# Moving the wo projection into the next unit's step, and cutting the last w2 rows into pieces of 5, 3 and 1

## Chip, cores, metric

One core of one Trainium2 chip. The metric is device time in microseconds (us) of one execution. The kernel before takes 137.39 us, the median of four runs between 137.38 and 137.50. The profile's span is 135.6 us; the rest lies outside it.

## The reference, cut to what matters

```python
xn = layernorm(x)                                   # x: 2 x 576
return x + attention(xn, k_cache, v_cache, wq, wo) + mlp(xn, w1, b1, w2, b2)

# attention: 32 query heads, 16 KV heads of 128, the last 2048 keys of the cache
# mlp: (relu(xn @ w1 + b1) ** 2) @ w2 + b2, hidden size 4608
```

Everything is bf16. One token for each of two sequences meets 53.6 MB of weights and cache: 16.8 MB each for K and V, 4.7 MB for wq and for wo, 5.3 MB for w1 and for w2.

## The kernel before

The work on the cache is cut into eight units (four KV heads of one sequence each). A unit is a step: 64 transposes of K on TensorE, copies of the transposed K out of PSUM, 64 score matmuls, a softmax over VectorE, GpSimd and ScalarE. PV of an earlier unit is mixed in. After two units (a head group) the wo projection follows: a select of eight matmuls and a sum of sixteen.

```python
    def wo_proj(tq):
        ...                                   # rr = oG * rmask; 8 select matmuls; ws = copy
        wo_sb = wo_tiles.pop(tq)
        for r in range(WR):                   # 8 rows, two matmuls each
            out_acc(ws[:, r, :], lambda a, z: wo_sb[:, r, a:z])

    def mlp_o(s, r0, r1, last=False):         # one w2 piece: two matmuls a row
        w2_sb = w2_tiles.pop((s, r0))
        for r in range(r0, r1):
            o = (r - r0) * D
            out_acc(mlp["h"][:, s * FR + r, :], lambda a, z: w2_sb[:, o + a:o + z], stop=...)

    W2P = [(0, 0, 9), (0, 9, 18), (1, 0, 9), (1, 9, 15), (1, 15, 18)]
    ...
    for u in range(2, NU + 2):
        if u < NU:
            step(u)
        else:
            for g in range(NG): pv(u - 2, g)
        ...
        if u - 2 >= 1 and (u - 2) % B == B - 1:
            wo_proj((u - 2) // B)
        ...                                   # load_v(u), wo, load_k(u + 2); w2 pieces at the last unit
    for i, w in enumerate(W2P):
        mlp_o(*w, last=(i == len(W2P) - 1))
    # cast of the PSUM sum to bf16, two stores
```

All loads but those of x, b1 and b2, which are small, go through one queue of the sync engine, in program order. K, V and w2 share a pool of six buffers, so a load waits for the last reader of the buffer that it takes (in the profiled run of the kernel before, the issues of K and V waited 17.0 us for transposes and 7.9 us for PV).

## Time and profile before

| | before |
|---|---|
| time, median of 4 | 137.39 us |
| span of the profiled run | 135.6 us |
| bytes by the load queue, rate from slice 2 to 37 | 53.61 MB, about 420 GB/s |
| last byte landed / final cast starts | 132.26 / 132.87 us |
| spread of the 16 completions of the last piece | 3.36 us |

The top of the page of the kernel before: busy time, share of the span and number of instructions of each engine, and the granted TensorE clock in tenths, in 40 slices of 3.4 us.

```profile
span 135.6 us, 4461 instructions
PE 102.5 (76%) x2054; PEld 91.9 (68%) x2054; DVE 53.9 (40%) x124; ACT 43.0 (32%) x47; POOL 10.0 (7%) x31
...
PEclk9999985569855685556985698698559959955599
```

No compute engine is full. A 76% busy TensorE with a mean granted clock of 0.76, which is half clock for about 48% of the span, is near enough to its limit to be watched. The DMA row, which the prediction shows, is full. The completion times in this text are the trace's semaphore updates. A load has 16 of them here, as many as the core has DMA engines. I read each as that of one engine; the records carry no engine number. A load counts as landed with the last: the last piece's 16 run from 128.90 to 132.26 us, and the first matmul on it begins at 132.30.

### The profile page before, as it was taken

The numbers are of one execution on the slowest core, as the hardware profiler recorded it, in microseconds if no ns is written. First come the engines' busy times: TensorE is split into PE (matmuls) and PEld (weight loads), VectorE is DVE, ScalarE is ACT, GpSimd is POOL, SyncE is SP. The second block draws the span as 40 slices with busy tenths as digits, with TensorE's granted clock in tenths as the row PEclk, the third lists the DMA queues.
The fourth block names the chain that finished last, engine by engine and source line by source line (L and its number), as shares of the span: only waits on it lengthen the run. The fifth ranks groups of instructions, "written<-read, shape, count | busy, mean of one in ns | idle before, by whom it ended". The sixth has DMA issues, their size and how long they took to land.

```text
span 135.6 us, 4461 instructions
## 1 busy us (share of the span) xinstructions
PE 102.5 (76%) x2054; PEld 91.9 (68%) x2054; DVE 53.9 (40%) x124; ACT 43.0 (32%) x47; POOL 10.0 (7%) x31
## 2 busy tenths in 40 slices
PE   1049947599968999879943993999399599768961
PEld 0039947589968999839933993688399479664530
DVE  7502421574352325422653446355634645660001
ACT  6705550165012521004701550272155127110000
POOL 6400000110110001100011001101100110110000
PEclk9999985569855685556985698698559959955599
DMA  5999999999999999999999999999999999999940
GB/s 112 418 419 418 428 442 402 420 429 440 430 393 430 438 411 409 444 425 396 440 440 406 445 420 425 404 443 423 425 430 413 430 415 426 422 410 417 393 166 1
DMA packets 5278, 53.90 MB, mean 397 GB/s; under 512 B 630, under 2 KB 652, under 8 KB 1164
## 3 DMA queue, kind: packets, MB, share of 16 engines
q1 hardware_dynamic: 5188, 53.61, 94.7%
q8 instruction: 16, 0.26, 0.8%
q0 software_dynamic: 64, 0.01, 0.0%
q14 instruction: 2, 0.02, 0.0%
q10 hardware_dynamic: 8, 0.00, 0.0%
HBM read 53.62 MB, written 0.00 MB: 395 GB/s over the span
## 4 chain that ended last, share of the span: by engine, by line
DMA 55%; PE 35%; DVE 3%; issue 2%; POOL 1%; ACT 1%; SPq 1%; POOLq 0%; ACTq 0%
DMA k<-in_A_k_cache_dram 41%; PE kT_ps L237 18%; DMA w<-in_B_w_dram 10%; PE hT_ps L323 5%; DMA b_sb<-in_B_b_dram 4%; PE sc_ps L252 4%; PE out_ps L213 4%; PE oT_ps L289 3%; PE qT_ps L225 1%; ACT kT L240 1%; POOL b_sb L146 1%; DVE l L271 1%; DVE sub L266 1%; SPq L94 0%; DVE fin_sb L414 0%
## 5 line engine op out<-in xcount | busy, mean ns | idle before, releaser
L237 PE MATMUL kT_ps<-ident,k 128*128 128x128 bf16 x512 | 47.3, 260 | 9.9 <-DMA k<-in_A_k_cache_dram 9.9
L237 PEld LDWEIGHTS <-k 128*128 128x128 bf16 x512 | 39.6, 119 | 11.8 <-DMA k<-in_A_k_cache_dram 10.7
L240 ACT COPY kT<-kT_ps 128x1024 bf16<-128x1024 bf16 x32 | 32.3, 1012 | 40.1 <-PE kT_ps L237 40.0
L242 DVE COPY kT<-kT_ps 128x1024 bf16<-128x1024 bf16 x32 | 22.0, 690 | 33.4 <-PE kT_ps L237 33.4
L252 PE MATMUL sc_ps<-qT_all,kT 128*128 128x8 bf16 x512 | 21.6, 168 | 1.6 <-ACT kT L240 0.8
L252 PEld LDWEIGHTS <-kT 128*128 128x128 bf16 x512 | 19.1, 100 | 2.6 <-ACT kT L240 1.2
L289 PE MATMUL oT_ps<-pT,v 128*128 128x8 bf16 x512 | 15.5, 167 | 1.9 <-issue 1.4
L269 ACT ACTIVATE pT<-sub 128x512 bf16<-128x512 f32 x8 | 5.0, 630 | 35.1 <-DVE sub L266 35.1
L289 PEld LDWEIGHTS <-v 128*128 128x128 bf16 x512 | 14.4, 99 | 2.1 <-issue 1.6
L271 DVE TENSOR_REDUCE l<-pT 128x8 f32<-128x512 bf16 x8 | 8.5, 1066 | 4.2 <-ACT pT L269 4.2
L213 PE MATMUL out_ps<-wo,ws 128*2 128x288 bf16 x64 | 8.3, 438 | 2.4 <-DVE ws L309 2.4
L323 PE MATMUL hT_ps<-xnT,w 128*128 128x2 bf16 x144 | 9.8, 201 | 0.0
L323 PEld LDWEIGHTS <-w 128*128 128x128 bf16 x144 | 9.4, 165 | 0.0
L258 DVE TENSOR_REDUCE m<-sc_ps 128x8 f32<-128x512 f32 x8 | 5.5, 692 | 9.7 <-PE sc_ps L252 9.7
L262 POOL PARTITION_ALL_REDUCE gmax<-m x8 | 2.9, 364 | 84.8 <-DVE m L260 84.8
L213 PE MATMUL out_ps<-w,hT_sb 128*2 128x288 bf16 x72 | 6.9, 353 | 1.3 <-DMA w<-in_B_w_dram 1.3
L213 PEld LDWEIGHTS <-ws 128*2 128x2 bf16 x64 | 3.5, 115 | 5.4 <-DVE ws L309 2.8
L213 PEld LDWEIGHTS <-hT_sb 128*2 128x2 bf16 x72 | 3.8, 103 | 4.3 <-issue 1.9
L266 DVE TENSOR_TENSOR sub<-sc_ps,gm 128x512 f32<-128x512 f32 x8 | 5.5, 692 | 0.3
L225 PE MATMUL qT_ps<-xnT,wq 128*128 128x2 bf16 x128 | 4.0, 165 | 2.2 <-DMA wq<-in_A_wq_dram 1.9
L225 PEld LDWEIGHTS <-wq 128*128 128x128 bf16 x128 | 3.9, 103 | 2.2 <-DMA wq<-in_A_wq_dram 2.0
L273 POOL PARTITION_ALL_REDUCE lsum<-l x8 | 3.2, 398 | 24.5 <-DVE l L271 24.5
(58 smaller groups left out, 35.1 us busy)
## 6 DMA issues: line engine op xcount, KB each, us to landing
v<-in_A_v_cache_dram SPq DMA_DIRECT2D x8, 2048.0 KB, 28.4
k<-in_A_k_cache_dram SPq DMA_DIRECT2D x7, 2048.0 KB, 29.4
w<-in_B_w_dram SPq DMA_DIRECT2D x4, 1152.0 KB, 17.7
wo<-in_A_wo_dram SPq DMA_DIRECT2D x4, 1152.0 KB, 27.4
wq<-in_A_wq_dram SPq DMA_DIRECT2D x4, 1024.0 KB, 6.9
w<-in_B_w_dram SPq DMA_DIRECT2D x3, 1296.0 KB, 22.7
k<-in_A_k_cache_dram SPq DMA_DIRECT2D x2, 1024.0 KB, 9.1
w<-in_B_w_dram SPq DMA_DIRECT2D x1, 864.0 KB, 15.7
```

What stands on the lines that cost most here:

```text
L213: nc.tensor.matmul(out_ps[32 * i:32 * i + B, :], lhsT=lhsT, rhs=rhs_of(i * OH, (i + 1) * OH), start=start, stop=stop, skip_group_check=True)
L225: nc.tensor.matmul(qT_ps[:, h, :], lhsT=lhsT, rhs=xnT[:, xc, :], start=(c == 0 and h == 0), stop=(c == KC - 1), skip_group_check=True)
L237: nc.tensor.transpose(out=kT_ps[:, i * P:(i + 1) * P], in_=k_sb[:, j * Dh:(j + 1) * Dh], identity=ident[:])
L240: nc.scalar.copy(out=kT[:], in_=kT_ps[:])
L242: nc.vector.tensor_copy(out=kT[:], in_=kT_ps[:])
L252: nc.tensor.matmul(sc_ps[:, g * JG + i, :], lhsT=kT[:, i * P:(i + 1) * P], rhs=qT_all[:, b, tq * NC:(tq + 1) * NC], start=True, stop=True)
L258: nc.vector.tensor_reduce(out=m1[:], in_=sc_ps[:].rearrange("p j c -> p c j"), axis=AX.X, op=ALU.max)
L266: nc.vector.tensor_tensor(out=sub[:], in0=sc_ps[:], in1=gm2[:].unsqueeze(1).to_broadcast([P, NJ, NC]), op=ALU.subtract)
L269: nc.scalar.activation(out=pT[:], in_=sub[:], func=ACT.Exp, scale=scale)
L271: nc.vector.tensor_reduce(out=l1[:], in_=pT[:].rearrange("p j c -> p c j"), axis=AX.X, op=ALU.add)
L289: nc.tensor.matmul(oT_ps[:], lhsT=v_sb[:, j * Dh:(j + 1) * Dh], rhs=pT_tiles[u][:, j, :], start=(j == 0), stop=(j == NJ - 1))
L323: nc.tensor.matmul(hT_ps[:, s * FR + r, :], lhsT=lhsT, rhs=xnT[:, xc, :], start=(c == 0 and s == 0 and r == 0), stop=(c == KC - 1), skip_g ...
```

## The change

Its intent is to take work off the end: the wo projection of a finished head group moves into a later step, the PV of the last units moves ahead of it, and the last loads become smaller, so that little is left to compute after the last byte. The core of the diff, with cuts marked:

```diff
-    W2P = [(0, 0, 9), (0, 9, 18), (1, 0, 9), (1, 9, 15), (1, 15, 18)]
+    W2P = [(0, 0, 9), (0, 9, 18), (1, 0, 9), (1, 9, 14), (1, 14, 17), (1, 17, 18)]
...
-    def wo_proj(tq):
+    def wo_sel(tq):            # the select; wo_acc(tq) has the 16 matmuls of the sum
...
-    def step(u, extra=()):
+    def step(u, hooks):
...
+            for f in hooks.get(g, ()):
+                f()
...
+    for u in range(2, NU):
+        hooks = {}
+        if u >= 4 and u % B == 0:
+            hooks = {3: [lambda t=u // B - 2: wo_sel(t)], 6: [lambda t=u // B - 2: wo_acc(t)]}
+        step(u, hooks)
...
+    for w in W2P:
+        issue_w2(*w)
+    for g in range(NG):
+        pv(NU - 2, g)
+    wo_sel(NQ - 2)
+    wo_acc(NQ - 2)
+    for g in range(NG):
+        pv(NU - 1, g)
+    mlp_o(*W2P[0])
+    wo_sel(NQ - 1)
+    mlp_o(*W2P[1])
+    wo_acc(NQ - 1)
+    for i in range(2, len(W2P)):
+        mlp_o(*W2P[i], last=(i == len(W2P) - 1))
```

Beside this the loads of b1 and b2 and the matmuls of x and b2 are written later, and a PSUM tile is cleared.

More of the change, by code (lines that the diff above doesn't have):

```diff
@@ L61 @@
     FR = L1 // P
-    NFC = S * FR
+    CH = [(s * L1 + r, FR, P) for s in range(S) for r in range(FR)]
+    NFC = len(CH)
     OH = D // 2
@@ L110, in issue_w1, with w_operands @@
         issue_w(w1_tiles, B_w1, c, "w1", F, L1)
-    def w_operands(tiles, c, col0, L, step=1):
-        last = col0 + (P - 1) * step
+    def w_operands(tiles, c, col0, L, step=1, m=P):
+        last = col0 + (m - 1) * step
         if c < NFULL:
@@ L144 @@
         issue_wq(c)
-    b1_sb = const.tile([P, S, FR], BF16, name="b1_sb")
-    nc.gpsimd.dma_start(out=b1_sb[:], in_=B_b1.rearrange("(s p r) -> p s r", s=S, p=P))
-    b2_sb = const.tile([1, D], BF16, name="b2_sb")
-    nc.gpsimd.dma_start(out=b2_sb[:], in_=B_b2.rearrange("(o n) -> o n", o=1))
     ones_f = const.tile([P, P], F32, name="ones_f")
@@ L214, in out_acc @@
                              start=start, stop=stop, skip_group_check=True)
-    out_acc(ident[:B, :B], lambda a, z: x_sb[:, a:z], start=True)
-    out_acc(ones_b[:, :], lambda a, z: b2_sb[:, a:z])
     qT_ps = psum.tile([P, Hq, B], F32, tag="misc", bufs=2, name="qT_ps")
@@ L295, in pv @@
             pT_tiles.pop(u)
-    def wo_proj(tq):
+    wo_state = {}
+    def wo_sel(tq):
         oG = oG_tiles.pop(tq)
@@ L309, in wo_proj, with wo_acc @@
         nc.vector.tensor_copy(out=ws[:], in_=wps[:])
+        wo_state[tq] = ws
+    def wo_acc(tq):
+        ws = wo_state.pop(tq)
         wo_sb = wo_tiles.pop(tq)
@@ L318, in mlp_h_block @@
             mlp["ps"] = psum.tile([P, NFC, B], F32, tag="misc", bufs=2, name="hT_ps")
+            nc.vector.memset(mlp["ps"][:], 0.0)
         hT_ps = mlp["ps"]
-        for s in range(S):
-            for r in range(FR):
-                lhsT, xc = w_operands(w1_tiles, c, s * L1 + r, L1, FR)
-                nc.tensor.matmul(hT_ps[:, s * FR + r, :], lhsT=lhsT, rhs=xnT[:, xc, :],
-                                 start=(c == 0 and s == 0 and r == 0), stop=(c == KC - 1), skip_group_check=True)
+        for i, (f0, step, m) in enumerate(CH):
+            lhsT, xc = w_operands(w1_tiles, c, f0, L1, step, m)
+            nc.tensor.matmul(hT_ps[0:m, i, :], lhsT=lhsT, rhs=xnT[:, xc, :],
+                             start=(c == 0 and i == 0), stop=(c == KC - 1), skip_group_check=True)
         if c == KC - 1:
@@ L327, in mlp_h_block @@
             nc.vector.tensor_tensor(out=t1[:], in0=hT_ps[:],
-                                    in1=b1_sb[:].rearrange("p s r -> p (s r)").unsqueeze(2).to_broadcast([P, NFC, B]),
+                                    in1=b1_sb[:].unsqueeze(2).to_broadcast([P, NFC, B]),
                                     op=ALU.add)
@@ L360 @@
     load_k(3)
-    nxt = {0: [], 1: [], 2: [lambda: load_v(2), lambda: load_k(4)]}
-    def step(u, extra=()):
+    def step(u, hooks):
         for g in range(NG + 2):
@@ L366, in step, with load_next @@
                 transposes(u, g)
-            if u >= 1 and 1 <= g <= NG:
-                if u >= 2:
-                    pv(u - 2, g - 1)
+            if u >= 2 and 1 <= g <= NG:
+                pv(u - 2, g - 1)
             if g >= 2:
                 scores(u, g - 2)
+            for f in hooks.get(g, ()):
+                f()
         softmax(u)
+    def load_next(u):
+        load_v(u)
+        if u % B == 0:
+            issue_wo(u // B)
+        if u + 2 < NU:
+            load_k(u + 2)
     for g in range(4):
@@ L384 @@
     softmax(0)
-    step(1)
+    b1_sb = const.tile([P, NFC], BF16, name="b1_sb")
+    nc.gpsimd.dma_start(out=b1_sb[:].rearrange("p (s r) -> p s r", s=S), in_=B_b1.rearrange("(s p r) -> p s r", s=S, p=P))
+    b2_sb = const.tile([1, D], BF16, name="b2_sb")
+    nc.gpsimd.dma_start(out=b2_sb[:], in_=B_b2.rearrange("(o n) -> o n", o=1))
+    step(1, {})
     mlp_h_block(0)
     mlp_h_block(1)
-    for u in range(2, NU + 2):
-        if u < NU:
-            step(u)
-        else:
-            for g in range(NG):
-                pv(u - 2, g)
+    out_acc(ident[:B, :B], lambda a, z: x_sb[:, a:z], start=True)
+    out_acc(ones_b[:, :], lambda a, z: b2_sb[:, a:z])
+    for u in range(2, NU):
[3 more added lines that the diff above has]
+        step(u, hooks)
         if u == 2:
@@ L396 @@
                 mlp_h_block(c)
-        if u - 2 >= 1 and (u - 2) % B == B - 1:
-            wo_proj((u - 2) // B)
-        if u < NU:
-            load_v(u)
-            if u % B == 0:
-                issue_wo(u // B)
-            if u + 2 < NU:
-                load_k(u + 2)
-        if u >= NU - 1:
-            pass
-        if u == NU - 1:
-            for w in W2P:
-                issue_w2(*w)
-    for i, w in enumerate(W2P):
-        mlp_o(*w, last=(i == len(W2P) - 1))
+        load_next(u)
+    for w in W2P:
[12 more added lines that the diff above has]
+        mlp_o(*W2P[i], last=(i == len(W2P) - 1))
     fin_sb = work.tile([32 + B, OH], BF16, tag="fin", name="fin_sb")
```

## The prediction

> **What bounds the kernel now.** I read the row of DMA load first, because 53.6 MB go through one core.
>
> ```profile
> DMA  5999999999999999999999999999999999999940
> GB/s 112 418 419 418 428 442 402 420 429 440 430 393 430 438 411 409 444 425 396 440 440 406 445 420 425 404 443 423 425 430 413 430 415 426 422 410 417 393 166 1
> ...
> q1 hardware_dynamic: 5188, 53.61, 94.7%
> q8 instruction: 16, 0.26, 0.8%
> ```
>
> From the second slice to the 38th all 16 DMA engines are busy, at about 420 GB/s. Moving 53.61 MB at that rate takes 127 to 128 us of a span of 135.6. TensorE is busy 76%, but wherever it waits, it waits for bytes. The chain that ended last says the same: 41% of the span is k transfers and 10% w transfers. So work that merely moves between earlier and later on TensorE is worth nothing unless it starves the DMA queue or lies after the last byte. Two places are left to look at.
>
> First, can the queue run empty? I added up what the sync engine had issued at each time and took off 0.42 MB for each us since 1.5 us. After the first microseconds the smallest surplus is 4.6 MB at 14.5 us (11 us of transfers), and from 16 us until only w2 is left it is never under 7.5 MB (18 us). Landing times of 27 to 29 us for most transfers fit. An issue that comes 6 us later costs nothing.
>
> Second, the end, in order of time:
>
> ```profile
> 119.21 0.33 SPq L129 DMA_DIRECT2D w<-in_B_w_dram  x1
> ...
> 119.69 1.87 PE L289 MATMUL oT_ps<-pT,v 128*128 128x8 bf16 x64 [0.51 <-ACT pT L269]
> ...
> 122.83 2.08 PE L213 MATMUL out_ps<-wo,ws 128*2 128x288 bf16 x16 [0.27 <-DVE ws L309]
> ...
> 124.70 4.18 PE L213 MATMUL out_ps<-w,hT_sb 128*2 128x288 bf16 x36
> ...
> 129.16 1.27 PE L213 MATMUL out_ps<-w,hT_sb 128*2 128x288 bf16 x18 [0.28 <-DMA w<-in_B_w_dram]
> ...
> 131.24 0.90 PE L213 MATMUL out_ps<-w,hT_sb 128*2 128x288 bf16 x12 [0.81 <-DMA w<-in_B_w_dram]
> ...
> 132.30 0.53 PE L213 MATMUL out_ps<-w,hT_sb 128*2 128x288 bf16 x6 [0.17 <-DMA w<-in_B_w_dram]
> ...
> 132.87 0.45 DVE L414 CAST fin_sb<-out_ps 34x288 bf16<-34x288 f32 x1 [10.10 <-PE out_ps L213]
> ```
>
> The last three w2 pieces (9, 6 and 3 rows, two matmuls a row) each wait for their bytes. After the last landing, at 132.26 us, only 0.57 us of matmuls and waits lie ahead of the final cast. That is the whole of what smaller last pieces can attack.
>
> The windows of the tail show something else:
>
> ```profile
> 126.00:128.00 2.00, 2.00 (x20) 1.07 (x18) 0.00 (x0) 0.00 (x0) 0.00 (x0) 0.50 0.99 408
> 128.00:129.00 1.00, 0.88 (x12) 0.43 (x7) 0.00 (x0) 0.00 (x0) 0.00 (x0) 0.81 0.83 332
> 129.00:130.00 1.00, 0.84 (x14) 0.61 (x15) 0.00 (x0) 0.00 (x0) 0.00 (x0) 1.00 0.58 227
> 130.00:131.00 1.00, 0.43 (x8) 0.17 (x3) 0.00 (x0) 0.00 (x0) 0.00 (x0) 1.00 0.48 183
> 131.00:132.00 1.00, 0.77 (x12) 0.52 (x12) 0.00 (x0) 0.00 (x0) 0.00 (x0) 1.00 0.32 124
> ```
>
> The last three columns are granted clock, DMA share and GB/s. The engines do not finish together. The completion records of the last piece run from 128.90 to 132.26 us: six engines are done by 129.24, eight only from 132.11 on. In the earlier records this spread is 0.3 us until 15.8 us, 1.8 us from 19.7 us and 3.3 us from 84.7 us. Each rise follows a 16 KB packet of the instruction queue (at 16.7 and 79.6 us; 16 such packets in all, of 1.06 us), and the next data packet on that engine is slow as well. My reading: 16 fetches fall on about eight engines, two each, at some 1.6 us a fetch. The number of TensorE instructions is equal in both kernels, so I leave this 3.3 us in place.
>
> [...] packets of 6912 and 3456 bytes take 0.2645 and 0.139 us, not quite a factor of two. [...] the trace shows 0.5 from 118.1 to 128.4 us and 1.0 up to 135.2.
>
> **The change, part by part.**
>
> *Pieces of 9, 5, 3, 1 rows in place of 9, 6, 3 at the end.* The landings were 129.12, 131.19 and 132.26: 2.07 us for 6 rows and 1.07 for 3, hence 0.333 us a row and 0.07 a piece (an estimate from two differences). The new ends: 5 rows at 129.12 + 0.07 + 1.67 = 130.86, 3 rows at 131.93, 1 row at 132.33, which is 0.07 later than before. On TensorE at full clock, 18, 12 and 6 matmuls took 1.27, 0.90 and 0.53 us: 0.062 us each and 0.16 [...]. Five rows: 130.90 to 131.68. Three rows: 131.97 to 132.50. One row: 132.37 + 0.28 = 132.65. Before it was 132.30 + 0.53 = 132.83. Gain 0.18 us, all on the path.
>
> *A sixth piece needs a sixth buffer.* Six slots rotate, so the one-row piece takes the slot of the last V and can be issued only after the last PV, near 121.6 us, where the last issue was at 119.21. It queues behind earlier bytes until 128 at least. Cost 0.
>
> *wo projection in the middle of the next unit's step.* Compiled order, kernel against kernel: the first two groups' select and sum move from ahead of a K unit's transposes to its last scores. The third moves from ahead of the last unit to the gap while the last softmax runs. Before, its 16 matmuls stood here, though by the landing records the last K was in at 107.05:
>
> ```profile
> 107.83 2.04 PE out_ps L213 x16
> 109.87 2.15 PE kT_ps L237 x24
> ```
>
> So the last unit can start 2.8 us sooner. But the last PV needs the last V, which lands at 119.64 us, and began at 119.69 already. Gain 0. The wo buffers come free some 6 us later, against a queue that still holds 15 us or more with them delayed. Cost 0.
>
> *PV of the sixth unit, counted from zero,* is now mixed into the last unit's scores; it only fills time before 119.64. Gain 0.
>
> *The last group's sum moves behind the first two w2 pieces.* Before, TensorE ran its 16 matmuls at 122.83, and the 36 after them kept it busy to 128.88, just ahead of the 129.12 landing. Now the first w2 piece runs at about 122.75, as it lands at 122.70, TensorE idles until the second lands at 125.94, then does 18, and then the 16. At half clock (4.18 / 36 = 0.116 us each) the 18 end at 128.07; the 16 take 1.0 to 1.9 us, to 129.1 to 129.9, around the third landing. With full clock from 128.4 as before, cost 0.
>
> *Start.* b1 and b2 loads are written later, yet the compiled order still has the b2 bias first on TensorE, and its load now stands behind the 0.97 us clearing of the select matrix. TensorE should begin Q about 1 us after the 9.23 us of before. The first issues that depend on it have 11 us or more of queued transfers ahead. Cost 0. One cleared PSUM tile on VectorE, under 0.4 us, lies beside other work.
>
> *Sum:* 137.40 - 0.18 = 137.2 us.
>
> **Rivals.** *The tail becomes TensorE's.* If the clock is 0.5 from 126 us to the end, the remaining 70 matmuls need 8.1 us from 125.98: done at 134.1, 1.45 us late, 138.7 us. For it: the moved sum leaves 3 us less work done early. Against it: with half clock until T and full after it, it binds only for T beyond about 131 (T + 4.34 - 0.534 (T - 126) = 132.65), and the half-clock stretches of the trace are 3.4 to 13.7 us long, so I give it one in five, usually with only part of the loss. *A starved queue* by the later wo buffers would show as gaps of 1 us or more, 138.5 or above; the 15 us of surplus speaks against it. *The stragglers change:* if moving instructions spared the late engines one fetch each, up to 1.6 us would go, 135.6; equal instruction counts speak against it. *The small piece costs more than 0.07 us* and eats the gain: 137.4.
>
> **Range and chances.** The sum is a small gain at the end; what could enlarge it is unlikely, and the late sum on TensorE pulls upward. So 137.2, with 136.6 to 138.2 for eight in ten. Two per cent is 2.75 us, more than any rival makes. Faster 0.01, same 0.97, slower 0.02.
>
> **What would show it.** Right: DMA still saturated to the 38th slice; last landing within 0.2 us of 132.3 with the spread near 3.3 us; two matmuls after it; the last PV again released by the last V near 119.6. Wrong: the last w2 piece landing long before its matmuls, TensorE without idle after 126 us, DMA tenths below 9 in the middle, or a last landing a microsecond away from 132.3.

The 0.16 us is the fixed rest of a straight line through the three groups (6, 12 and 18 matmuls in 0.53, 0.90 and 1.27 us), an estimate. "Wherever it waits, it waits for bytes" is too strong: in the profiled run the listed waits of TensorE are 18.3 us for DMA and 10.6 us for other engines. A fetch is a 16 KB packet of q8, the queue of kind "instruction". The slow data packet after it is seen by its time alone: the 16 fetches took 1.02 to 1.11 us each, and within 0.02 us of the end of each a data packet begins that takes 0.46 to 0.55 us longer than the median of its size (after the sixteenth 0.24 us), in eleven cases one of 16 KB with 1.08 to 1.16 us in place of 0.61. That it is on the same engine is my reading. A fetch and what the packet loses come to about 1.6 us, an estimate from these figures.

## The result, and the profile after

The kernel after takes 137.21 us (four runs, 137.10 to 137.33) against 137.39. Ratios here are the mean time of one kernel's fast runs over that of the other's of the same rounds, so not quite the ratio of the medians quoted. The ratio is 0.9985, with a 95% interval of 0.9968 to 1.0003. Measured again in the last batch it was 0.9987 (0.9974 to 0.9999). That is a gain of 0.2 us, "same" at a threshold of 2%.

The DMA rows of the page of the kernel after:

```profile
DMA  3999999999999999999999999999999999999940
GB/s 126 401 427 426 426 438 409 415 439 436 411 420 408 439 421 426 415 431 411 436 431 426 421 431 416 406 450 411 436 421 423 425 411 437 416 406 423 393 177 1
...
q1 hardware_dynamic: 5332, 53.61, 94.4%
q8 instruction: 16, 0.26, 0.8%
```

Full to the 38th slice again, the same bytes, 16 instruction packets again. The new pieces show as 144 more packets on q1. So the queue never starved, although wo loads were issued later, as the sync engine's records show, first before, then after (start, duration, instruction):

```profile
61.11 0.33 SPq L123 DMA_DIRECT2D wo<-in_A_wo_dram  x1
...
86.76 0.33 SPq L123 DMA_DIRECT2D wo<-in_A_wo_dram  x1
```

```profile
70.60 0.33 SPq L124 DMA_DIRECT2D wo<-in_A_wo_dram  x1
...
95.16 0.33 SPq L124 DMA_DIRECT2D wo<-in_A_wo_dram  x1
```

That is 9.5 and 8.4 us later, and no gap follows in the GB/s row. The tail of the kernel after, in order of time:

```profile
119.73 1.87 PE L282 MATMUL oT_ps<-pT,v 128*128 128x8 bf16 x64 [0.44 <-DMA v<-in_A_v_cache_dram]
...
126.02 2.32 PE L209 MATMUL out_ps<-w,hT_sb 128*2 128x288 bf16 x18 [0.82 <-DMA w<-in_B_w_dram]
...
128.13 2.04 PE L209 MATMUL out_ps<-wo,ws 128*2 128x288 bf16 x16
...
130.01 1.88 PE L209 MATMUL out_ps<-w,hT_sb 128*2 128x288 bf16 x28
132.04 0.65 PE L209 MATMUL out_ps<-w,hT_sb 128*2 128x288 bf16 x8 [0.16 <-DMA w<-in_B_w_dram]
...
132.74 0.45 DVE L424 CAST fin_sb<-out_ps 34x288 bf16<-34x288 f32 x1 [9.99 <-PE out_ps L209]
```

The last PV is released by the last V, at 119.73 us where it was 119.69: all that the reordering moved forward ended in this wait. Before, two things came at the same time there: the prediction's line for that PV names the last softmax (`pT`), and the line of its weight load, below, names V, whose landing was at 119.64 us.

```profile
119.69 1.79 PEld L289 LDWEIGHTS <-v 128*128 128x128 bf16 x64 [0.59 <-DMA v<-in_A_v_cache_dram]
```

In the kernel after, the softmax is done at 118.73 us, where it was 119.64, and V alone is left. The last three landings are 130.90, 132.00 and 132.37 us. The eight matmuls of the last two pieces run in one go, and the cast begins 0.37 us after the last landing, where before it was 0.61. The last landing itself is 0.11 us later in this pair of profiled runs.

The windows of the tail (busy time of each engine, then granted clock, DMA share and GB/s):

```profile
128.00:129.00 1.00, 1.00 (x12) 0.55 (x10) 0.00 (x0) 0.00 (x0) 0.00 (x0) 0.50 0.80 310
129.00:130.00 1.00, 1.00 (x12) 0.53 (x8) 0.00 (x0) 0.00 (x0) 0.00 (x0) 0.52 0.67 255
130.00:131.00 1.00, 1.00 (x22) 0.71 (x18) 0.00 (x0) 0.00 (x0) 0.00 (x0) 1.00 0.42 165
```

Two things are to be seen. The clock stayed at half until nearly 130 us, so TensorE was busy without a gap from 126.02 to 131.89 us and was ready only 0.15 us ahead of the next piece. And the DMA share falls off over four microseconds as before: completions of the last piece run from 128.90 to 132.37 us.

### The profile page after: what moved, and what is told of

It is laid out like the page before. It is cut to its first block, busy times and chain, and to the rows that moved or that the text cites. A ratio compares the mean times of both kernels' runs of the same rounds, so it can differ in the third digit from the quotient of the medians.

```text
span 135.4 us, 4461 instructions
## 1 busy us (share of the span) xinstructions
PE 102.7 (76%) x2054; PEld 93.3 (69%) x2054; DVE 53.7 (40%) x125; ACT 42.8 (32%) x47; POOL 9.9 (7%) x31
## 4 chain that ended last, share of the span: by engine, by line
DMA 69%; PE 23%; DVE 3%; POOL 2%; issue 1%; ACT 0%; SPq 0%; POOLq 0%
DMA k<-in_A_k_cache_dram 41%; DMA w<-in_B_w_dram 24%; PE kT_ps L230 13%; DMA b_sb<-in_B_b_dram 4%; PE sc_ps L245 3%; PE oT_ps L282 3%; PE out_ps L209 2%; PE qT_ps L218 1%; DVE l L264 1%; POOL b_sb L391 1%; POOL sel L197 1%; DVE sub L259 1%; ACT pT L262 0%; DVE kT L235 0%; DVE fin_sb L424 0%
## 5 line engine op out<-in xcount | busy, mean ns | idle before, releaser
L230 PE MATMUL kT_ps<-ident,k 128*128 128x128 bf16 x512 | 49.7, 267 | 13.9 <-DMA k<-in_A_k_cache_dram 13.6
L230 PEld LDWEIGHTS <-k 128*128 128x128 bf16 x512 | 41.0, 122 | 14.6 <-DMA k<-in_A_k_cache_dram 14.3
L245 PE MATMUL sc_ps<-qT_all,kT 128*128 128x8 bf16 x512 | 22.1, 168 | 2.8 <-ACT kT L233 1.4
L245 PEld LDWEIGHTS <-kT 128*128 128x128 bf16 x512 | 20.0, 102 | 4.2 <-ACT kT L233 1.8
L282 PE MATMUL oT_ps<-pT,v 128*128 128x8 bf16 x512 | 16.3, 167 | 0.4 <-DMA v<-in_A_v_cache_dram 0.4
L209 PE MATMUL out_ps<-wo,ws 128*2 128x288 bf16 x64 | 6.8, 359 | 0.3 <-DVE ws L304 0.3
## 6 DMA issues: line engine op xcount, KB each, us to landing
k<-in_A_k_cache_dram SPq DMA_DIRECT2D x7, 2048.0 KB, 26.3
```

The source lines that it names most:

```text
L209: nc.tensor.matmul(out_ps[32 * i:32 * i + B, :], lhsT=lhsT, rhs=rhs_of(i * OH, (i + 1) * OH), start=start, stop=stop, skip_group_check=True)
L230: nc.tensor.transpose(out=kT_ps[:, i * P:(i + 1) * P], in_=k_sb[:, j * Dh:(j + 1) * Dh], identity=ident[:])
L245: nc.tensor.matmul(sc_ps[:, g * JG + i, :], lhsT=kT[:, i * P:(i + 1) * P], rhs=qT_all[:, b, tq * NC:(tq + 1) * NC], start=True, stop=True)
L282: nc.tensor.matmul(oT_ps[:], lhsT=v_sb[:, j * Dh:(j + 1) * Dh], rhs=pT_tiles[u][:, j, :], start=(j == 0), stop=(j == NJ - 1))
```

## The experiments

Theory: the time is that of the last byte plus what is computed after it; the pieces give the whole gain, the new order gives nothing, and the last byte is 3.4 us late because eight of the sixteen DMA engines each served two instruction fetches. Rivals: the reordering makes the gain; TensorE has time to spare in the tail; the engines are late for reasons of their own.

The table collects what the traces say of the tail, in us. "Late group" is the number of DMA engines whose completion of the last piece falls in the last 0.5 us (in the kernel after no slow data packet follows the sixteenth fetch, at 129.9 us; my reading is that it hit an engine that had almost finished, hence 7 for 8).

| kernel | last landing | spread | late group | cast after last landing |
|---|---|---|---|---|
| before | 132.26 | 3.36 | 8 | 0.61 |
| after | 132.37 | 3.48 | 7 | 0.37 |
| after, measured again | 132.44 | 3.50 | 7 | 0.37 |
| old pieces, three runs | 132.92, 132.72, 132.10 | 4.16, 3.79, 3.31 | | 0.62, 0.62, 0.74 |
| new pieces only, two runs | 133.38, 132.91 | 4.35, 3.55 | | 0.37, 0.37 |
| sum first | 133.36 | 4.29 | | 0.37 |
| sum late | 132.78 | 3.69 | | 1.73 |
| few instructions | 130.82 | 1.76 | 6 | 0.40 |
| thin PV | 132.34 | 3.44 | 5 | 0.37 |

### Pieces or order: old pieces on the new order

```diff
-    W2P = [(0, 0, 9), (0, 9, 18), (1, 0, 9), (1, 9, 14), (1, 14, 17), (1, 17, 18)]
+    W2P = [(0, 0, 9), (0, 9, 18), (1, 0, 9), (1, 9, 15), (1, 15, 18)]
```

> The kernel after with the last pieces of 9, 6 and 3 rows again, all else (order, loads) as after. My theory (the whole gain of 0.18 us is the shorter work after the last landing): 137.4 us, the same as before within 0.1; last landing 132.2 to 132.4, then 6 matmuls for about 0.53 us and the final cast at 132.8 to 133.0. Rival (the gain came from the moved wo projection and PV): 137.2, and the cast not later than in the kernel after (132.74).

Measured in the first batch: 138.13 us, ratio 1.0016 (0.998 to 1.0051). The kernel before itself ran between 137.36 and 138.21 us in that batch, so the time decides nothing. Its start moved fewer bytes than usual (391 and 381 GB/s in slices 2 and 3 of its page; 418 and 419 in the kernel before, 401 and 427 in the kernel after); why, is not shown. The trace decides more: the cast starts 0.62 us after the last landing, as in the kernel before, in spite of the new order.

> The same kernel as in the run with the old pieces of 9, 6 and 3 rows, since the chip of that call gave two levels of times 0.8 us apart. On a chip whose runs of the kernel before agree within 0.3 us: 137.4, ratio to before 0.999 to 1.001, cast about 0.6 us after the last landing. Rival (the reordering makes the gain): ratio 0.998 to 0.999.

Again a noisy batch (before: 137.29 to 138.04): 138.03 us, ratio 1.0026 (1.0003 to 1.0049), outside both expectations; cast 0.62 us after the last landing.

> The kernel after with pieces of 9, 6 and 3 rows, third time. My theory (pieces alone make the gain, the new order is worth nothing): ratio to before 0.9995 to 1.0005 and 0.1 to 0.3 us above the kernel after of the same call. Rival (the new order costs something, as the two noisy calls hint with 1.0016 and 1.0026): ratio 1.0015 or more, and more than 0.3 us above the kernel after.

> The kernel after itself, beside the one with the old pieces, since the two earlier calls were too noisy for 0.2 us. My theory: ratio to before 0.998 to 0.999 if the runs of before agree within 0.3 us; cast 0.35 to 0.4 us after the last landing. Rival (no gain at all; the 0.18 us of the first measurement was chance): ratio 0.9995 to 1.001.

This last batch was quiet, with ten of the eleven runs of the kernel before between 137.29 and 137.47 us. Old pieces: 137.38 us, ratio 1.0003 (0.999 to 1.0017). Kernel after: 137.18 us, ratio 0.9987. On one chip, with the order the same, the medians stand 0.20 us apart, which is what the new pieces are worth (old pieces 137.30 to 137.76, new ones 137.14 to 137.39, so the ranges still overlap). For the new order with old pieces no gain is seen, to within the interval of about 0.2 us to either side, which is as wide as the gain itself. Single traces decide less: between these two profiled runs the last landing differs by 0.34 us (132.10 and 132.44), where the smaller pieces were estimated at 0.07. The profile of the run with old pieces shows how near TensorE was to being the bound:

```profile
129.84 2.96 PE L209 MATMUL out_ps<-w,hT_sb 128*2 128x288 bf16 x36
132.84 0.45 DVE L424 CAST fin_sb<-out_ps 34x288 bf16<-34x288 f32 x1 [10.29 <-PE out_ps L209]
```

The last 36 matmuls ran without a wait and ended after the last landing at 132.10 by more than their own six need, 0.74 us in place of 0.62. In this run the granted clock was 0.50 until 131.0 us (0.99 from 131 to 132), just the limit that the prediction had worked out.

### Pieces or order: new pieces on the old order

```diff
-    W2P = [(0, 0, 9), (0, 9, 18), (1, 0, 9), (1, 9, 15), (1, 15, 18)]
+    W2P = [(0, 0, 9), (0, 9, 18), (1, 0, 9), (1, 9, 14), (1, 14, 17), (1, 17, 18)]
```

> The kernel before with nothing changed but the last pieces of 9, 5, 3 and 1 rows. My theory: the full gain, 137.1 to 137.25 us, final cast near 132.7; TensorE idle for some tenths ahead of the third and fourth piece, since the last group's sum is done early. Rival (the reordering makes the gain): 137.4.

> The same kernel as in the run with the new pieces alone on the order of before, again for the noise. My theory: 137.1 to 137.25, ratio 0.998 to 0.999, cast about 0.37 us after the last landing. Rival: 137.4, ratio 1.000.

Both runs fell into the noisy batches: 137.94 us, ratio 1.0002 (0.9973 to 1.0031), and 137.63 us, ratio 0.999 (0.9969 to 1.0011). Both medians miss the 137.1 to 137.25 us that I gave; the second ratio lies in its range. In both traces the cast starts 0.37 us after the last landing, the figure of the kernel after. The second one's tail has the waits that the new order lost:

```profile
131.46 0.78 PE L213 MATMUL out_ps<-w,hT_sb 128*2 128x288 bf16 x10 [0.48 <-DMA w<-in_B_w_dram]
132.57 0.67 PE L213 MATMUL out_ps<-w,hT_sb 128*2 128x288 bf16 x8 [0.33 <-DMA w<-in_B_w_dram]
```

So one line of the diff makes the whole gain that the tail shows after the last landing, and without using up TensorE's slack. Its gain in time was not measured alone in a quiet batch. In the two noisy batches old pieces on the new order came out 0.1 and 0.4% above new pieces on the old one. The pieces account for 0.15%; whether the new order costs something on top when the start is disturbed stays open. The quiet batch shows no such cost.

### The place of the last group's sum

Sum ahead of the first w2 piece:

```diff
-    mlp_o(*W2P[0])
     wo_sel(NQ - 1)
-    mlp_o(*W2P[1])
     wo_acc(NQ - 1)
-    for i in range(2, len(W2P)):
+    for i in range(len(W2P)):
```

> The kernel after, with the sum of the last head group ahead of the first w2 piece, as in the kernel before. My theory: no change from after, 137.1 to 137.25 us, but idle time of TensorE ahead of the w2 landings after 126 us comes back (about 1 us in sum), where the kernel after had none between 126.0 and 131.9. Rival (the sum placed behind the second w2 piece is part of the gain, since it fills a wait): slower than after by 0.1 us or more.

138.17 us, ratio 1.002 (0.999 to 1.005), in the first noisy batch; the time is open. The trace has the expected idle time back: TensorE waited 1.32, 0.45 and 0.34 us ahead of the last three groups, and the cast came 0.37 us after the last landing. The first of them:

```profile
130.20 1.27 PE L209 MATMUL out_ps<-w,hT_sb 128*2 128x288 bf16 x18 [1.32 <-DMA w<-in_B_w_dram]
```

Sum one piece later:

```diff
     mlp_o(*W2P[1])
+    mlp_o(*W2P[2])
     wo_acc(NQ - 1)
-    for i in range(2, len(W2P)):
+    for i in range(3, len(W2P)):
```

> The kernel after, with the sum of the last head group one piece later, behind the third w2 piece. My theory: the kernel after had only about 0.15 us of slack on TensorE in the tail, so this goes over it: TensorE idles about 1 us before the third piece lands at 129.2, and the last matmuls start after their bytes have landed. 137.5 to 138.1 us with half clock until 130 us, 137.2 to 137.4 if the clock is full from 128.4. Rival (TensorE has a microsecond or more to spare in the tail): 137.2 whatever the clock.

139.21 us, ratio 1.0113 (1.0066 to 1.0159): slower by far more than the noise, and by more than I expected. In the tail TensorE first idles, then is late:

```profile
129.61 2.32 PE L209 MATMUL out_ps<-w,hT_sb 128*2 128x288 bf16 x18 [0.88 <-DMA w<-in_B_w_dram]
...
131.72 1.64 PE L209 MATMUL out_ps<-wo,ws 128*2 128x288 bf16 x16
...
133.20 1.27 PE L209 MATMUL out_ps<-w,hT_sb 128*2 128x288 bf16 x18
```

The last 18 matmuls, for bytes that had landed by 132.78, end near 134.5 us. Sixteen matmuls in the wrong place cost more than the whole change gained, and the rival of a microsecond to spare falls.

### What the last byte waits for: fewer instructions

The edit, abridged. The copies of the transposed K, which the cut leaves out, are each split in two, because a PSUM tile now has half the columns.

```diff
-        for i in range(JG):                       # 8 transposes
-            nc.tensor.transpose(out=kT_ps[:, i*P:(i+1)*P], in_=k_sb[:, j*Dh:(j+1)*Dh], identity=ident[:])
+        nc.tensor.matmul(kT_ps[:], lhsT=ident[:], rhs=k_sb[:, <512 columns>], start=True, stop=True)
...
-        for i in range(JG):                       # 8 score matmuls of 8 columns
+        nc.tensor.matmul(sc_ps[<64 columns>], lhsT=kT[:, 0:P], rhs=<qT_all, 64 columns>, start=True, stop=True)
...
+            if i not in (0, JG - 1):              # PV: two of eight
+                continue
```

> Wrong result on purpose: the kernel after with one wide matmul for each group of eight transposes and of eight score matmuls, and PV thinned to two of eight. 1550 TensorE instructions in place of 4110, bytes unchanged. My theory: about 6 instruction fetches in place of 16, no engine hit twice, spread of the last completion 1.8 us in place of 3.5, last landing 1.5 us earlier, 135.5 to 135.9 us. Rival (the engines are late for a reason of their own): 16 KB instruction packets fall to 6 and the spread stays at 3.3 us, 137.1.

136.04 us, ratio 0.9903 (0.989 to 0.9915), in a batch whose runs of the kernel before lay between 137.22 and 137.50. The median is 0.1 us above the range that I gave; the profiled run, 135.77, is the fastest of the four. Instruction packets from its page, and the end of its tail:

```profile
q8 instruction: 6, 0.10, 0.3%
```

```profile
130.52 0.66 PE L209 MATMUL out_ps<-w,hT_sb 128*2 128x288 bf16 x8 [0.32 <-DMA w<-in_B_w_dram]
```

The bytes of the load queue are unchanged, and the earliest engine finishes the last piece at 129.07 us, not before the 128.90 of the kernel after. The latest finishes at 130.82 in place of 132.37. The spread halves, 1.76 for 3.48 us, and six engines fall in the last 0.5 us, as many as there were fetches. This is what "two fetches an engine become one" says, and the rival of engines late for their own reasons falls.

### Only PV thinned

```diff
+            if i not in (0, JG - 1):
+                continue
             nc.tensor.matmul(oT_ps[:], lhsT=v_sb[...], rhs=pT_tiles[u][:, j, :], ...)
```

> Wrong result on purpose: the kernel after with only PV thinned to two matmuls of eight, 3342 TensorE instructions. My theory: about 13 fetches, five engines still hit twice, so the end stays where it is: 137.0 to 137.2 us (TensorE has more slack), spread 3.3 to 3.6 us, but fewer engines in the last group (about five in place of eight). Rival (the lateness goes with the number of instructions or with TensorE's use of SBUF): spread down by a fifth, to 2.8 us, and the time 0.6 us shorter.

137.32 us, 0.1 above my range, ratio 0.9994 (0.998 to 1.0009); spread 3.44 us, five engines in the late group.

```profile
q8 instruction: 13, 0.21, 0.6%
```

Thirteen fetches over eight engines leave five that are hit twice and three that are hit once, and this is what the completion records of the last piece count: eight engines are done by 130.05 us, three from 130.49 to 130.59, five from 132.02 to 132.34. So each fetch costs its engine about 1.6 us, an estimate from these levels. The packets of the trace carry no engine number; that the late engines are those that were hit is read from the times and from these counts. A fifth fewer fetches gained nothing in the landing (132.34 us): the worst engine counts, not the sum.

### Two attempts to even out the engines

If eight engines are late, bytes might be given to the others. Both attempts use loads with a small slowest source dimension: those with 8 had eight completions each in the trace, the one with 4 had four, where the other loads of the queue have 16. "Low" in the expectations names the eight or four engines that the author took these loads to run on; no run here shows which engines they were. The 26.3 GB/s an engine is an estimate: about 420 GB/s of the page over 16 engines. First attempt, one V tile by four loads, two of them with a slowest source dimension of 8:

```diff
+        nc.sync.dma_start(out=tl[0:64, :], in_=v[0:16, :, :])
+        nc.sync.dma_start(out=tl[64:128, n:], in_=v[16:32, :, n:])
+        nc.sync.dma_start(out=tl[64:96, 0:n], in_=v[16:24, :, 0:n])
+        nc.sync.dma_start(out=tl[96:128, 0:n], in_=v[24:32, :, 0:n])
```

> The kernel after, with one V tile (the fourth) loaded by four transfers in place of one: two of them cover 32 partitions whose slowest source dimension is 8, [...] so that 655 KB go over 8 engines and not over 16: 1.56 us more work for the low eight and 1.56 us less for the others (at 26.3 GB/s an engine). My theory (the end is set by about eight engines that are 3.3 us late through instruction fetches): if those are the eight high ones, the last landing comes 1.3 to 1.6 us earlier and the time is 135.6 to 136.0 us with a spread under 1 us; if they are among the low ones, the last landing comes about 1.5 us later, 138.7 us, and the spread grows to about 6.4 us (the low ones) or 4.9 (mixed). Rival (the spread is no fixed set of engines, or the end is set by the total of the bytes): 137.2 within 0.2.

146.59 us, ratio 1.0686. None of the three expectations came. The two loads had eight completions each, but from 72 to 84 us the rate was halved, 202 to 227 GB/s, while the engines counted as busy, a DMA share of 0.96 to 1.05:

```profile
76.00:80.00 4.00, 4.00 (x73) 4.00 (x71) 1.54 (x3) 2.60 (x3) 0.00 (x0) 0.69 1.05 227
80.00:84.00 4.00, 1.99 (x48) 1.73 (x46) 2.28 (x6) 1.27 (x2) 0.36 (x1) 1.00 1.04 219
```

Packets of 16 KB took about 1.2 us in place of 0.61. The first two of the four loads each write one half of the partitions, and the expectation left this out of account; whether that is the cause is not shown. The slowdown hides the 1.56 us in question, so this run says nothing on the question that it was made for.

Second attempt, on all 128 partitions: part of a wq tile with its rows in another order, so that the slowest source dimension is 4 (the normalised x gets a matching copy).

```diff
+        rows = A_wq[c * P:(c + 1) * P, :]
+        nc.sync.dma_start(out=tl[:, 0:XH * Dh], in_=rows.rearrange("(b a) n -> a b n", a=4)[:, :, 0:XH * Dh])
+        nc.sync.dma_start(out=tl[:, XH * Dh:Hq * Dh], in_=rows[:, XH * Dh:])
```

> The kernel after with 328 KB of the fourth wq tile (10 heads of columns, rows stored in another order on all 128 partitions) loaded by a transfer whose slowest source dimension is 4. [...] The other twelve engines save 328 KB / 16 / 26.3 GB/s = 0.78 us each, the low four take 2.3 us more. My theory (the end is the end of the engines hit by two fetches): last landing 0.7 to 0.8 us earlier at about 131.6 and 136.3 to 136.7 us, spread 2.5 to 2.8 us; if one of the low four is among the late, last landing 2.3 us later and 139.4 us. Rival (total bytes set the end): 137.2 within 0.15.

140.76 us, ratio 1.0228, in the second noisy batch, but far outside its noise; last landing 135.63, spread 4.3 us. The result is correct, and none of the numbers expected fits: the last landing is 3.3 us later, not 2.3. While those 328 KB went in, everything slowed:

```profile
16.00:19.00 3.00, 1.34 (x40) 1.25 (x39) 0.73 (x2) 2.11 (x2) 0.00 (x0) 1.00 1.02 214
19.00:22.00 3.00, 0.00 (x0) 0.00 (x0) 0.00 (x0) 0.00 (x0) 0.00 (x0) 0.67 1.11 247
```

Packets of 4 KB of other loads took 0.32 us at that time, 0.16 in the kernel after. Why a transfer with four completions goes with slower loads beside it is not shown. That the late engines lie outside these four was a guess; which ones they are stays open too. No correct version that beats the kernel after came out of this; the new pieces on the old order are as good by their tail, with more slack.

## Why the prediction was right

**The total.** Predicted 137.2, measured 137.21 and 137.18 us. That it agrees to 0.02 us is luck: the interval of the ratio is 0.2 us to either side.

**The term of the sum.** I had the three last landings at 130.86, 131.93 and 132.33 us; they came at 130.90, 132.00 and 132.37. I had the end of the matmuls at 132.65; the cast began at 132.74, its wait included. The gain of 0.18 us as the sum of a later byte and a shorter remainder is what the batch with both kinds of pieces measured (0.20 us). In the two first traces the terms are a byte 0.11 us later and a remainder 0.24 us shorter, so the cast moved by 0.13 us: the shorter remainder is the term that every trace with the new pieces shows (but for the run with the sum one piece later), while the later byte scatters from run to run. Two readings of the kernel before were slightly off without consequence: from the last landing to the cast it is 0.61 us and not 0.57, and the first w2 piece landed at 122.79 us and not 122.70.

**The terms of zero.** The last PV was bound by the last V, the later wo loads left no gap, and the sixth piece, with its late buffer, arrived in order. Right, though wo was issued 8 to 10 us later and not "some 6": the queue still covered it. By the prediction's own sum (bytes issued, less 0.42 MB a us), the kernel after had 6.4 and 5.7 MB left at these two issues, about 15 and 14 us of transfers (an estimate).

**The instruction fetches.** Argued from one trace then, supported now by two runs: with six fetches the last landing is 130.82 us, 1.5 us earlier than in the kernel after, with thirteen it is 132.34, and the late group goes with the count of fetches (seven with 16 and five with 13, by my reading hit twice each; six with six, hit once each). The fetches go with the TensorE instructions: 16, 13 and 6 for 4110, 3342 and 1550.

**The start.** Wrong in its size: I expected Q about 1 us later. From the kernel after:

```profile
0.72 0.95 POOL L197 MEMSET sel<- 128x1024 bf16 x1 [0.29 <-POOLq L441]
...
9.31 0.99 PE L218 MATMUL qT_ps<-xnT,wq 128*128 128x2 bf16 x32 [0.26 <-DVE xnT L186]
```

Q begins 0.08 us later than the 9.23 of before. The clearing runs at 0.72 us, in time in which GpSimd had been idle before its first load at 1.28. It cost nothing in either case.

**The tail on TensorE.** I assumed full clock from 128.4 us and got half clock to 129.95. My formula put the limit at 131, so the end held, but the margin was 0.15 us. "TensorE without idle after 126 us" stood in my list of signs of a wrong prediction. It happened, and the prediction was right all the same: the sign should have been a matmul that starts after its bytes. The run with the sum one piece later shows the kind of loss that I gave one chance in five. What makes the clock half or full is not shown by the busy time of the profile. In the kernel before, 13.6 us ran at half clock with TensorE busy for 12.21 us of it, and half clock followed right after 6.7 us at full clock with 6.32 us busy:

```profile
49.90:63.50 13.60, 12.21 (x212) 10.89 (x212) 4.45 (x12) 1.64 (x2) 0.76 (x2) 0.50 1.01 422
111.40:118.10 6.70, 6.32 (x172) 5.91 (x169) 3.65 (x7) 3.57 (x4) 0.36 (x1) 1.00 1.02 426
```

## What to carry to other kernels

Here the DMA row was full from slice 2 to 38, and the reordering of compute showed no gain (ratio 1.0003 with old pieces); the gain lay after the last byte. In such a kernel measure the time from the last landing to the end first, and cut that with smaller last pieces, here 0.24 us of it for 0.11 us of later landing in the first pair of traces and 0.2 us in all. Check what the reordering takes away, too: work moved behind a late load uses up slack which the profile doesn't call a cost, and one piece further it cost 1%. Look at the completions one by one: the cast came 0.37 to 0.74 us after the last of the 16 in every run of the table but the one with the sum late, and here, by my reading of the counts, the program's own instruction stream made eight engines late (last landing 132.37 us with 16 fetches, 130.82 with six).
